# Third group of the first token part's first MLP: its in-projections by seven block products instead of eight

## The chip, the cores and the metric

The kernel runs on one core of one Trainium2 chip. The metric is the device time of one execution in microseconds (us); the median of three runs of the kernel before is 928.54 us. On the core TensorE (PE) multiplies, VectorE (DVE), ScalarE (ACT) and GpSimd (POOL) work element by element, and SyncE (SP) issues the transfers between HBM and the on-chip memory.

## The reference

Causal attention with a window of 128 (4 sequences, 8 heads, 576 positions, head dimension 64) gives 2304 tokens of 512 features; two MLPs follow, and all of it is in float32:

```python
x = attn(q, k, v)                       # 2304 x 512
g = x @ w_gate; v = x @ w_val           # 512 -> 1536
x = (g * sigmoid(g) * v) @ w_out1       # 1536 -> 512
h = x @ w_in                            # 512 -> 2048
out = (h * sigmoid(h)) @ w_out2         # 2048 -> 512
```

## The kernel before, in words

**Precision.** Every float32 operand is kept as a high and a low half in a rounded float32 format, and each product is three matmuls (high x high, high x low, low x high; L905, L906 and L907 in `passes` for the in-projections, L1188 to L1190 for the first MLP's out-projection, L1221 to L1223 for the second's). A *split* makes the halves: one rounding copy (L348 on ACT or L349 on DVE) and one subtraction (L357 on DVE or L358 on POOL).

**Tiling.** The tokens are taken in three parts of 6 tiles of 128 (768 tokens, two halves of N = 384). The hidden features of the first MLP are taken in `G1` = 6 groups of 256, those of the second in `G2` = 8 groups. A group of the first MLP has an in-projection of `w_gate` and one of `w_val`, an activation, and an out-projection that is added into `ACC`.

**Two ways for an in-projection.** With features and tokens each cut in two, the product of a group is a 2 x 2 by 2 x 2 block product.

- `moe1_plain` and `plain` do all eight block products. They read the operand slots 0 to 3 of `XOP`, which hold the plain token blocks, and four weight units per matrix. Blocks of tokens can be done as they come.
- `moe1` and `quad` do seven (the Strassen-Winograd form, products A11, S2, S1, A12, S3, S4, A22). They need slots 4, 5 and 6 of `XOP`, which hold sums and differences of blocks, and slot 1 holds a difference in place of its plain block. They need seven weight units per matrix, four of them splits of sums made by `strassen_sums` (tile `sums`). Three banks of partial results are also copied and added to one another while the products run (`copy` is L348 into `tmp`, `add_to` is L951, the fourth block is L966).

Before the first `quad` of a part, `operands` makes those slots (L695 differences into PSUM banks, then splits into `XOP`). In part 0 the attention writes `XOP` straight, so `restore` first adds the halves back into `XST` (L357 or L358, `XST<-XOP`), eight times 128x384.

**Weights.** `raw_weight` loads 512 KB of a weight matrix as it lies in HBM into one of two staging buffers `raw0`, `raw1` (L754); ACT takes some bits out of it (L755, into the single tile `top`), DVE joins them into float32 (L758, into one of three tiles `word`). Only then is the staging buffer free for the next load. A group takes six such loads (two each for `w_gate`, `w_val`, `w_out1`). Made units (ring of 17, `wu`) are stored to HBM (L772, `kept_g`, `kept_v`) so that later parts fetch them: in `quad_weights`, mode `raw` loads and makes all seven units and stores them; mode `sum` fetches the three units and two float32 words that a plain group stored, makes the other four and stores those; mode `kept` fetches all seven.

**Order of the work.** A planner (`Plan`) records every operation with a cost, a due time and its dependences, and then issues them engine by engine from this cost table; PSUM banks are handed out by it too (a bank of kind "B" for the differences, "mm" for products). Each engine, and SP for transfers, works off its list in that order. Part 1's attention is planned into the time of part 0's MLPs.

The number of plain groups is `GP`; it is used in these lines only:

```python
    moe1_plain(range(1, GP))
    restore(state["t"] - 10000.0)
    operands(XST, "xt", state["t"], plain=False)
    t_moe2 = t_next - 6000.0 + (G1 - GP) * 22 * pe_cost(6, N) + (GP - 1) * 24 * pe_cost(6, N)
    moe1(0, range(GP, G1), "raw", True)
    moe1(1, range(GP), "sum", True)
    moe1(1, range(GP, G1), "kept", True)
            if part == 1 and GP - 1 <= g < G1 - 1:
                out_sums(*jobs.pop(0), t0, gw["A22"][1])
```

`out_sums` makes, in part 1, weight sums that part 2 uses for its out-projections; there are 11 jobs, 3 of them in the first MLP with `GP` = 3 and the other 8 in the second.

Of the kernel before, what the change touches and what calls it, by code (L numbers as in the profile page):

```python
# [201 lines left out]
def attention_moe_moe2_kernel(  # L202
# [43 lines left out]
    NP = H // 2  # L246
    G1, G2 = F1 // (2 * P), F2 // (2 * P)
    EARLY = 6
    GP = 3
    NU, NO, NRAW, NW, NH, NTMP = 17, 3, 2, 3, 6, 8  # L250

    big = ctx.enter_context(tc.tile_pool(name="big", bufs=1))
# [114 lines left out]
    def pe_cost(count, n):  # L367
        return count * max(n * PE_COL + PE_MM, PE_MIN)
# [292 lines left out]
    def restore(due):  # L661

        for j in range(2):
            for blk in range(2):
                for kk in range(2):
                    c, slot = 2 * j + kk, x_slot(j, blk)
                    hi, lo = (tiles(XOP[:, slot, i, kk].bitcast(F32)) for i in range(2))
                    dst = XST[:, blk * BT:blk * BT + BT, c, :]
                    sum_op(
                        N, due, lambda dst=dst: dst, lambda hi=hi: hi, lambda lo=lo: lo, ALU.add,  # L670
                        x_keys(slot, kk), [("xt", blk * BT + t, c) for t in range(BT)],
                    )
# [175 lines left out]
    def out_weight(kind, f, first, due, load_due=None):  # L848
        i = take("o", NO)
        t, ok = O_W[i], ("o", i)  # L850
        if first:
            w, wk = raw_weight(kind, f, due if load_due is None else load_due, due + 8000.0)
            split_weight(t, ok, w, [wk], KC * P, due + 8000.0)
            store(KEPT[kind][f], flat(t), ok, ("kept", kind, f), due + 8000.0, 1460.0)
        else:
            fetch(KEPT[kind][f], flat(t), ok, ("kept", kind, f), due, 1460.0)
        return t, ok

    def out_sums(kind, g, due, behind):

        a = {}
        for j in range(2):
            n = take("word", NW)
            w, wk, low = W_R[n], ("word", n), TOP_R[0].bitcast(F32)
            for dst, dk, part in ((w, wk, 0), (low, "top", 1)):
                src = KEPT["o" + kind][2 * g + j][:, KC * P * part:KC * P * (part + 1)]
                plan.add(
                    "sp", 730.0, due + 1800.0 * j, lambda src=src, dst=dst: nc.sync.dma_start(out=dst, in_=src),
                    [("kept", "o" + kind, 2 * g + j), behind], [dk],
                )  # L870
            sum_op(KC * P, due, lambda w=w: w, lambda w=w: w, lambda low=low: low, ALU.add, ["top"], [wk])
            for i in range(2):
                a[i, j] = (w[:, 2 * P * i:2 * P * i + 2 * P], [wk])
        for n, (t, tk) in enumerate(strassen_sums(a, due, LATE)):
            m = take("stage", len(STAGE))
            u, uk = STAGE[m][0], ("stage", m)
            split_weight(u, uk, t, tk, 2 * P, due, before.pop(uk, ()), LATE)
            store(KEPT["s" + kind][g, n], lambda u=u: flat(u()), uk, ("kept", "s" + kind, g, n), due, 730.0)
# [365 lines left out]
    def flush():  # L1244
        for fn, c in pend:
            fn(state["t"])
            state["t"] += c
        pend.clear()
# [4 lines left out]
    def attention_part(part, at):  # L1253
        for i in range(part * PT, part * PT + PT):
            load(i, "k", at(i) - 14820.0)
            load(i, "q", at(i) - 20070.0)
            load(i, "v", at(i) - 7670.0)
            for halves in [(0,), (1,)] if i < EARLY else [(0, 1)]:
                t0 = at(i + 0.5 * halves[0])
                for hf in halves:  # L1260
                    prepare(i, hf, t0 - 8000.0)
                banks = score(i, halves, t0)
                for hf in halves:
                    attend(i, hf, [at(i + p / NP) for p in (2 * hf, 2 * hf + 1)], banks[hf])
                weigh(i, halves, at(i + 0.5 * halves[-1] + 1 / NP))
# [4 lines left out]
    def moe1_plain(groups):  # L1270
        for g in groups:
            if g == 0:

                gw = plain_weights("g", 0, -220.0, 26910.0)
                vw = plain_weights("v", 0, 880.0, 28010.0)
                ws = [out_weight("o1", i, True, 29750.0 - 8000.0 + 550.0 * i, 1980.0 + 550.0 * i) for i in range(2)]
                blocks = ((0, 2), (2, 2), (4, 2))
            else:
                t0 = state["t"] - WLEAD
                gw = plain_weights("g", g, t0, t0 + 8000.0)  # L1280
                vw = plain_weights("v", g, t0 + 5000.0, t0 + 5000.0 + 8000.0)
                ws = None
                blocks = ((0, BT), (BT, BT))
            for blk in blocks:
                hs = []
                n = blk[1] * P
                for i in range(2):
                    cg = plain(gw, i, blk, state["t"])
                    cv = plain(vw, i, blk, state["t"])
                    state["t"] += pe_cost(24, n)  # L1290
                    if i == 0:
                        flush()
                    if ws is None:
                        ws = [out_weight("o1", 2 * g + i, True, t0 + 12000.0 + 550.0 * i) for i in range(2)]
                    hs.append(hidden1(cg, cv, n, True, state["t"]))
                for d in range(KC):
                    pend.append((lambda due, a=(g, ws, d, blk, hs): out1(*a, due), pe_cost(6, n)))

    def moe1(part, groups, mode, psum):
        for g in groups:  # L1300
            t0 = state["t"]
            gw = quad_weights("g", g, mode, t0 - WLEAD)
            vw = quad_weights("v", g, mode, t0 - WLEAD + 7300.0)
            cg, state["t"] = quad(gw, state["t"])
            flush()
            if part == 2 and g < G1 - 1:
                units = out_units("1", g, t0 - WLEAD + 15000.0)
                cv, state["t"] = quad(vw, state["t"])
                hs = late_hidden(value1(cg, cv, state["t"]), state["t"])
                for name in ORDER_OUT:  # L1310
                    for d in range(2):
                        pend.append((lambda due, a=(g, units, hs, name, d): late_out1(*a, due), pe_cost(3, N)))
                continue
            if part == 2:
                combine(state["t"])
            ws = [out_weight("o1", 2 * g + i, part == 0, t0 - WLEAD + 15000.0) for i in range(2)]
            if part == 1 and GP - 1 <= g < G1 - 1:
                out_sums(*jobs.pop(0), t0, gw["A22"][1])
            cv, state["t"] = quad(vw, state["t"])
            hs = {}  # L1320
            for i, b in ((0, 0), (0, 1), (1, 1), (1, 0)):
                hs[i, b] = hidden1(cg[i, b], cv[i, b], N, psum, state["t"])

            for b in (1, 0):
                for d in range(KC):
                    pend.append((
                        lambda due, a=(g, ws, d, (b * BT, BT), [hs[0, b], hs[1, b]]): out1(*a, due), pe_cost(6, N),
                    ))
# [33 lines left out]
    def spread(part, t0, span):  # L1362
        attention_part(part, lambda x: t0 + (x - part * PT) / PT * span)
# [3 lines left out]
    t_next = state["t"] + 6000.0  # L1367
# [5 lines that stand above are left out]
    early = lambda x: t_next + 0.0 + (x - PT) * 33000.0  # L1373
    attention_part(1, lambda x: early(x) if x < PT + PT // 2 else t_moe2 + 20000.0 + (x - PT - PT // 2) * 33000.0)
    moe1(0, range(GP, G1), "raw", True)
    flush()
# [4 lines left out]
    spread(2, state["t"] + 6000.0, M1 + M2 - 28000.0)  # L1381
    moe1(1, range(GP), "sum", True)
    moe1(1, range(GP, G1), "kept", True)
    flush()
# [44 lines left out]
```

## Time and profile before

| | us |
|---|---|
| runs | 927.59, 928.54 (median), 932.44 |
| profiled execution, span from first to last instruction | 929.4 |
| PE busy | 909.7 (98%) |
| DVE busy | 703.4 (76%) |
| ACT busy | 529.8 (57%) |
| POOL busy | 529.0 (57%) |
| DMA, mean over the span | 260 GB/s |

Of the profiled execution the page gives the span, 929.4 us; it stands 0.9 us above the median of the runs. Matmuls overlap, so the mean duration of one (some 333 ns at 384 columns) is longer than the distance from one start to the next. PE is busy nearly all the time, so what a change does is read from PE's own work, from the few stretches in which PE is idle, and from the granted clock of TensorE (PEclk; 1.0 is 2.4 GHz, 0.5 is 1.2 GHz). In the trace part 0's first MLP runs as follows on PE: group 0 from 27 to 80 us, interleaved with the attention; group 1 to 103; group 2 (the third) to 135; groups 3, 4 and 5 to 157, 186 and 212.

### The profile page before, as it was taken

How to read it: one execution, taken by the hardware profiler on the slowest of the kernel's cores; microseconds unless marked ns; L12 is line 12 of the kernel's file. 1: busy time of each engine (PE TensorE's matmuls, PEld its weight loads, DVE VectorE, ACT ScalarE, POOL GpSimd, SP SyncE). 2: the span in 40 equal slices, each digit the busy share in tenths (PEclk: the TensorE clock that was granted, in tenths of full speed). 3: DMA queues.
4: the chain of work that ended last, by engine and by line, in shares of the span. 5: the costliest groups of instructions: out<-in, count | busy, mean ns of one | idle time of the engine just before them, and what ended most of it. 6: DMA issues, size and time to landing. Idle time of an engine off the chain costs nothing.

```text
span 929.4 us, 17799 instructions
## 1 busy us (share of the span) xinstructions
PE 909.7 (98%) x5758; PEld 845.7 (91%) x5758; DVE 703.4 (76%) x1623; ACT 529.8 (57%) x1362; POOL 529.0 (57%) x613
## 2 busy tenths in 40 slices
PE   7999999999999999999999999999999999999998
PEld 5889899997988888999999989889899999999997
DVE  7888869878989788748576977576755776868885
ACT  6887567767977685754343575445354333474431
POOL 2766377777656669675331555464344445687454
PEclk9999999999999999999999999999999999999999
DMA  9989796898888987999878787979888887587702
GB/s 226 268 236 279 251 318 210 291 304 282 272 277 284 293 293 273 331 321 309 270 246 251 251 272 272 335 268 304 287 303 249 254 250 254 190 254 229 221 24 91
DMA packets 181677, 241.58 MB, mean 260 GB/s; under 512 B 68048, under 2 KB 97232, under 8 KB 181584
## 3 DMA queue, kind: packets, MB, share of 16 engines
q1 hardware_dynamic: 181584, 240.44, 80.1%
q8 instruction: 46, 0.75, 0.3%
q14 instruction: 47, 0.39, 0.1%
HBM read 169.61 MB, written 70.78 MB: 259 GB/s over the span
## 4 chain that ended last, share of the span: by engine, by line
PE 74%; DVE 8%; POOL 6%; DMA 6%; issue 3%; ACT 2%; SPq 0%; POOLq 0%; DVEq 0%; ACTq 0%
PE bank L905 14%; PE bank L906 13%; PE bank L907 13%; PE bank L1221 5%; PE bank L1222 5%; PE bank L1223 5%; PE bank L493 3%; PE bank L607 3%; PE bank L1189 2%; PE bank L1188 2%; PE bank L1190 2%; PE bank L570 2%; POOL h L358 1%; PE bank L1121 1%; PE bank L1122 1%
## 5 line engine op out<-in xcount | busy, mean ns | idle before, releaser
L905 PE MATMUL bank<-XOP,wu 128*128 128x384 f32 (+1 forms) x868 | 297.3, 343 | 4.7 <-ACT tmp L348 1.5
L906 PE MATMUL bank<-XOP,wu 128*128 128x384 f32 (+1 forms) x868 | 289.4, 333 | 1.2 <-DVE XOP L357 0.6
L907 PE MATMUL bank<-XOP,wu 128*128 128x384 f32 (+1 forms) x868 | 289.3, 333 | 0.0
L905 PEld LDWEIGHTS bank<-XOP,wu 128*128 128x128 f32 x868 | 163.5, 188 | 14.4 <-ACT tmp L348 3.8
L906 PEld LDWEIGHTS bank<-XOP,wu 128*128 128x128 f32 x868 | 163.6, 189 | 3.5 <-DVE XOP L357 1.4
L907 PEld LDWEIGHTS bank<-XOP,wu 128*128 128x128 f32 x868 | 163.3, 188 | 0.1
L348 ACT ACTIVATE tmp<-bank 128x384 f32<-128x384 f32 x134 | 62.7, 489 | 66.0 <-PE bank L907 39.7
L358 POOL TENSOR_TENSOR h<-tmp,h 128x384 fp32r<-128x384 f32 x48 | 50.6, 1063 | 65.4 <-ACT h L348 64.3
L1221 PE MATMUL bank<-wo,h 128*128 128x512 f32 (+1 forms) x218 | 87.1, 400 | 0.1
L1223 PE MATMUL bank<-wo,h 128*128 128x512 f32 (+1 forms) x218 | 85.6, 393 | 0.0
L1222 PE MATMUL bank<-wo,h 128*128 128x512 f32 (+1 forms) x218 | 85.5, 392 | 0.0
L1233 DVE TENSOR_TENSOR ACC<-bank,ACC 128x512 f32<-128x512 f32 (+1 forms) x97 | 64.6, 681 | 17.3 <-PE bank L1223 16.6
L358 POOL TENSOR_TENSOR wu<-word,wu 128x256 fp32r<-128x256 f32 x63 | 50.7, 819 | 44.0 <-ACT wu L348 38.8
L553 POOL TENSOR_TENSOR cs<-cs,st 128x512 f32<-128x512 f32 x36 | 39.5, 1096 | 62.7 <-DVE st L550 45.5
L1188 PE MATMUL bank<-h,wo 128*128 128x384 f32 (+1 forms) x216 | 73.1, 338 | 0.1
L1189 PE MATMUL bank<-h,wo 128*128 128x384 f32 (+1 forms) x216 | 71.9, 333 | 0.9 <-POOL h L358 0.6
L951 DVE TENSOR_TENSOR bank<-bank,tmp 128x384 f32<-128x384 f32 x93 | 52.3, 562 | 26.7 <-PE bank L907 23.6
L1190 PE MATMUL bank<-h,wo 128*128 128x384 f32 (+1 forms) x216 | 71.6, 332 | 0.0
L1018 ACT ACTIVATE tmp<-bank 128x384 f32<-128x384 f32 (+1 forms) x121 | 57.3, 483 | 22.6 <-PE bank L907 10.4
L1029 DVE SCALAR_TENSOR_TENSOR bank<-tmp,bank 128x384 f32<-128x384 f32 (+1 forms) x98 | 52.7, 549 | 21.1 <-ACT tmp L1018 12.0
L348 ACT ACTIVATE h<-bank 128x384 fp32r<-128x384 f32 (+1 forms) x95 | 45.8, 484 | 39.2 <-DVE bank L1029 23.9
L758 DVE SCALAR_TENSOR_TENSOR word<-raw,top 128x512 int32<-128x512 int32 x68 | 57.8, 849 | 11.1 <-ACT top L755 10.0
(413 smaller groups left out, 2169.2 us busy)
## 6 DMA issues: line engine op xcount, KB each, us to landing
wu<-kept_i SPq DMA_DIRECT2D x112, 256.0 KB, 3.6
wu<-kept_g SPq DMA_DIRECT2D x72, 256.0 KB, 4.2
wu<-kept_v SPq DMA_DIRECT2D x72, 256.0 KB, 4.4
wo<-kept_o SPq DMA_DIRECT2D x34, 512.0 KB, 4.8
raw<-in_moe_w_out_dram SPq DMA_DIRECT2D x28, 512.0 KB, 4.9
kept_o<-wo SPq DMA_DIRECT2D x28, 512.0 KB, 4.2
kept_i<-wu SPq DMA_DIRECT2D x56, 256.0 KB, 3.2
kept_s<-later_raw SPq DMA_DIRECT2D x44, 256.0 KB, 4.3
```

The source lines that it names most:

```text
L348: act = lambda: nc.scalar.activation(out(), src(), AF.Copy)
L358: pool = lambda: nc.gpsimd.tensor_tensor(out(), x(), y(), op)
L905: nc.tensor.matmul(ps, wh, xh, start=start, stop=False, skip_group_check=True)
L906: nc.tensor.matmul(ps, wh, xl, start=False, stop=False, skip_group_check=True)
L907: nc.tensor.matmul(ps, wl, xh, start=False, stop=stop, skip_group_check=True)
L1188: nc.tensor.matmul(ps[:, 0:n], wh, h[:, 0], start=(i == 0), stop=False)
L1189: nc.tensor.matmul(ps[:, 0:n], wh, h[:, 1], start=False, stop=False)
L1190: nc.tensor.matmul(ps[:, 0:n], wl, h[:, 0], start=False, stop=(i == 1))
L1221: nc.tensor.matmul(ps, hh, wh, start=(i == 0), stop=False)
L1222: nc.tensor.matmul(ps, hh, wl, start=False, stop=False)
L1223: nc.tensor.matmul(ps, hl, wh, start=False, stop=(i == 1))
L1233: plan.add("dve", cost("dve", n), due, lambda: nc.vector.tensor_tensor(acc, pv(), acc, ALU.add), [b], keys, give=b)
```

## The change

`GP` goes from 3 to 2.

```diff
     G1, G2 = F1 // (2 * P), F2 // (2 * P)
     EARLY = 6
-    GP = 3
+    GP = 2
     NU, NO, NRAW, NW, NH, NTMP = 17, 3, 2, 3, 6, 8
```

So group 2 of part 0 goes through `moe1` with mode `raw` instead of `moe1_plain`; `restore` and `operands` of part 0 are due one group earlier; group 2 of part 1 uses mode `kept` instead of `sum`; the second half of part 1's attention is due a little earlier (`t_moe2`); and in part 1 one `out_sums` job moves from the second MLP to group 1 of the first. Everything is planned anew from there. Up to 77 us of the trace before the lists are the same but for some bank numbers; three places behind that follow. In them `h` is a group's activation, `wo` its out-projection weights, `cs` the attention's scores.

PE, from the end of group 1 to group 2; of each product or pair of products the first row. Before:

```order
L570 MATMUL bank7_135<-ident_67,cs_120 128x128 x4
L1188 MATMUL bank0_128<-h0_100,wo2_92 128x384
L1188 MATMUL bank1_129<-h0_100,wo2_92 128x384
L905 MATMUL bank4_132<-XOP_63,wu14_87 128x384
L905 MATMUL bank5_133<-XOP_63,wu16_89 128x384
L905 MATMUL bank7_135<-XOP_63,wu3_76 128x384
L1188 MATMUL bank0_128<-h2_102,wo2_92 128x384
```

And now:

```order
L570 MATMUL bank0_128<-ident_67,cs_120 128x128 x4
L1188 MATMUL bank5_133<-h0_100,wo2_92 128x384
L1188 MATMUL bank1_129<-h0_100,wo2_92 128x384
L905 MATMUL bank5_133<-XOP_63,wu14_87 128x384
L905 MATMUL bank1_129<-XOP_63,wu16_89 128x384
L905 MATMUL bank4_132<-XOP_63,wu0_73 128x384
L905 MATMUL bank3_131<-XOP_63,wu1_74 128x384
L905 MATMUL bank4_132<-XOP_63,wu3_76 128x384
L905 MATMUL bank3_131<-XOP_63,wu4_77 128x384
L905 MATMUL bank4_132<-XOP_63,wu5_78 128x384
L1188 MATMUL bank2_130<-h2_102,wo2_92 128x384
```

The first half of group 1's out-projection starts in bank 5 instead of bank 0, and the seven gate products of group 2 (wu16 and wu0 to wu5) stand where four plain products stood.

DVE, at the making of slots 4 to 6. Before:

```order
L695 TENSOR_TENSOR bank4_132<-XST_64 128x384
L695 TENSOR_TENSOR bank6_134<-XST_64,bank0_128 128x384
L349 CAST XOP_63<-bank0_128 128x384
L357 TENSOR_TENSOR XOP_63<-bank0_128,XOP_63 128x384
L357 TENSOR_TENSOR XOP_63<-bank6_134,XOP_63 128x384
L695 TENSOR_TENSOR bank3_131<-XST_64,bank4_132 128x384
```

And now:

```order
L357 TENSOR_TENSOR wo0_90<-word2_98,wo0_90 128x512
L695 TENSOR_TENSOR bank6_134<-XST_64 128x384
L758 SCALAR_TENSOR_TENSOR word2_98<-raw0_93,top0_95 128x512
L357 TENSOR_TENSOR XOP_63<-bank1_129,XOP_63 128x384
L357 TENSOR_TENSOR XOP_63<-bank2_130,XOP_63 128x384
L695 TENSOR_TENSOR bank7_135<-XST_64,bank5_133 128x384
```

The last row, which now stands behind the conversion of a `w_val` load and two splits, is the last reader of bank 5.

ACT, behind the loads of `w_out1`. Before (the loads of group 2's second half of `w_out1` and of group 3's `w_gate`):

```order
L755 ACTIVATE top0_95<-raw1_94 128x512
L348 ACTIVATE h3_103<-bank4_132 128x384
L1018 ACTIVATE tmp2_108<-bank5_133 128x384
L755 ACTIVATE top0_95<-raw0_93 128x512
L348 ACTIVATE wu7_80<-word0_96 128x256
L348 ACTIVATE wu10_83<-word0_96 128x256
L348 ACTIVATE h4_104<-bank7_135 128x384
```

And now (the first row is that of group 2's second half of `w_out1`):

```order
L755 ACTIVATE top0_95<-raw1_94 128x512
L348 ACTIVATE wu11_84<-sums_99 128x256
L348 ACTIVATE tmp2_108<-bank1_129 128x384
L348 ACTIVATE h3_103<-bank5_133 128x384
L348 ACTIVATE tmp3_109<-bank4_132 128x384
L348 ACTIVATE tmp4_110<-bank3_131 128x384
L1018 ACTIVATE tmp2_108<-bank1_129 128x384
L755 ACTIVATE top0_95<-raw0_93 128x512
```

The copies of the first seven-product form (`tmp2`, `tmp3`, `tmp4`) stand behind the bits of that load, and the bits of group 3's `w_gate` behind them.

## Rows read from the trace of the kernel before

**Rows 1.** The page: span, and each engine's busy time, share, instructions.

```profile
span 929.4 us, 17799 instructions
PE 909.7 (98%) x5758; PEld 845.7 (91%) x5758; DVE 703.4 (76%) x1623; ACT 529.8 (57%) x1362; POOL 529.0 (57%) x613
```

**Rows 2.** PE's waits over the span: us in total, times, longest.

```profile
PE bank L570 <- DVE ACC L1205: 1.4, 1, 1.4
PE bank L905 <- DVE bank L695: 1.3, 1, 1.3
PE bank L453 <- DVE KR L448: 1.2, 1, 1.2
PE bank L905 <- DVE tmp L966: 0.8, 1, 0.8
```

**Rows 3.** Stretches: length, busy PE PEld DVE ACT POOL (count), PEclk, DMA share, GB/s.

```profile
80.00:103.00 23.00, 23.00 (x165) 22.56 (x164) 21.63 (x46) 14.23 (x37) 13.88 (x16) 1.00 0.80 251
103.00:135.00 32.00, 30.43 (x189) 29.16 (x188) 20.20 (x38) 18.55 (x40) 19.91 (x25) 0.95 0.91 299
157.00:186.00 29.00, 28.25 (x200) 27.01 (x199) 26.54 (x64) 21.07 (x56) 21.95 (x27) 1.00 0.92 292
352.00:640.00 288.00, 285.73 (x1788) 264.87 (x1788) 202.11 (x484) 151.38 (x403) 153.37 (x193) 1.00 0.85 285
```

**Rows 4.** The chain that ended last, 103 to 113 us: start, length, what.

```profile
103.14 5.68 DMA raw<-in_moe_w_gate_dram
...
108.91 0.80 ACT top L755
...
109.78 0.70 DVE word L758
...
110.51 0.72 ACT wu L348 x2
...
111.64 0.57 DVE h L357
```

**Rows 5.** PE in order of time: start, duration, [idle before]; products of 384 columns.

```profile
111.46 0.66 PE L570 MATMUL bank<-ident,cs 128*128 128x128 f32 x4 [1.44 <-DVE ACC L1205]
...
114.70 0.52 PE L906 MATMUL bank<-XOP,wu 128*128 128x384 f32 x1
115.02 0.52 PE L907 MATMUL bank<-XOP,wu 128*128 128x384 f32 x1
...
134.68 0.33 PE L905 MATMUL bank<-XOP,wu 128*128 128x384 f32 x1
...
135.72 0.33 PE L905 MATMUL bank<-XOP,wu 128*128 128x384 f32 x1
```

**Rows 6.** PE in order of time, the end of the last attention tile in group 0.

```profile
83.64 0.33 PE L907 MATMUL bank<-XOP,wu 128*128 128x384 f32 x1
...
94.15 0.42 PE L1188 MATMUL bank<-h,wo 128*128 128x384 f32 x1
```

**Rows 7.** DVE in order of time.

```profile
83.71 0.42 DVE L635 TENSOR_TENSOR XOP<-bank,XOP 128x256 fp32r<-128x256 f32 x1 [0.18 <-ACT XOP L348]
...
85.85 1.50 DVE L758 SCALAR_TENSOR_TENSOR word<-raw,top 128x512 int32<-128x512 int32 x1
...
90.58 1.20 DVE L695 TENSOR_TENSOR bank<-XST 128x384 f32<-128x384 f32 x1
91.70 0.55 DVE L695 TENSOR_TENSOR bank<-XST,bank 128x384 f32<-128x384 f32 x1
```

**Rows 8.** POOL in order of time, the same stretch.

```profile
85.80 1.01 POOL L358 TENSOR_TENSOR XST<-XOP 128x384 f32<-128x384 f32 x1
...
89.37 1.99 POOL L358 TENSOR_TENSOR XST<-XOP 128x384 f32<-128x384 f32 x2
```

**Rows 9.** Groups by form over the span: busy us, mean ns, idle before.

```profile
L358 POOL TENSOR_TENSOR wu<-sums,wu 128x256 fp32r<-128x256 f32 x78 | 61.4, 816 | 1.4 <-ACT wu L348 1.1 <-DMA kept_v<-wu 0.3
L951 DVE TENSOR_TENSOR bank<-bank,tmp 128x384 f32<-128x384 f32 x93 | 52.3, 562 | 26.7 <-PE bank L907 23.6 <-ACT later_raw L348 1.4 <-ACT tmp L348 0.7
```

## The prediction

> **What bounds the kernel now.** I read the page first: PE is busy for 909.7 of 929.4 us, no other engine for more than 76% [rows 1]. The time is PE's own work, and some 20 us in which it waits. So I listed PE's waits next. Apart from the start, where the first load is awaited, only four have more than 0.7 us: 1.4, 1.3, 1.2 and 0.8 us [rows 2]. Then the stretches group by group: from 80 to 103 us PE is full and DVE nearly is (21.63 of 23 us); from 103 to 135 us, the third group, PE is idle for 1.57 us and the granted clock is 0.95 in the mean [rows 3]. In part 1 (352 to 640 us) PE is busy for 285.73 of 288 us [rows 3], so little can be won there.
>
> The wait of the third group lies at 111.46 us: PE idles 1.44 us, and the matmuls after it start 0.32 us apart (114.70, 115.02) where later ones need 1.04 us for six, 0.173 us each (134.68 to 135.72) [rows 5]. That is the lower level of TensorE's clock, 1.2 GHz in place of 2.4 GHz, after an idle engine. The chain tells what PE waited for. A load of `w_gate` for group 3, which nobody needs before 135 us, takes 5.68 us; then ACT takes its bits (0.80) and DVE joins them (0.70); only behind these stand ACT's copies and the last step of `h`, which PE needs [rows 4]. Urgent work stood behind a conversion of weights that were not urgent.
>
> **The change part by part.**
>
> *Matmuls.* Eight block products per matrix become seven. A block product is 2 x 3 matmuls of 384 columns, and there are two matrices: 12 matmuls fewer, at 0.173 us [rows 5]. PE is full around them, so all of it counts: **-2.1 us**.
>
> *The old wait and its slow clock.* In the new lists of PE and ACT (the change, above) the seven gate products, 7.3 us of PE work, stand where this wait came up, and the activation that was awaited there no longer exists in that place. I take the 1.44 us as gone. The slow clock costs (1 - 0.95) x 32 = 1.6 us [rows 3]. Together **-3.0 us**; the other bound is 0, if a wait as long takes its place.
>
> *The end of the last attention tile.* Six products of 384 columns (1.04 us) that covered the wait for DVE's last low half now come later. That half ends at 83.71 + 0.42 us; on the new list DVE has one restoring addition and one difference more ahead of it, while POOL has one addition less, so some 0.4 us later, 84.5 us. PE is there at 83.64 + 0.17 = 83.8 us [rows 6, 7]: **+0.7 us**, between 0 and 1.5.
>
> *The bank of the differences.* Group 1's first out-projection opens bank 5. Its last reader is now DVE's difference for slot 4. I laid DVE's list after 84.5 us row by row (0.34 us for 256 columns, 0.47 for 384, 0.6 to 0.7 for 512, from starts in [rows 7]; waits for ACT where ACT's list is longer): that difference ends at about 96 us. PE came there at 94.15 us [rows 6], and with 0.7 us of delay at 94.9 us. **+1.0 us**; if nothing on DVE is late it is 0, and if each difference there needs 1.20 instead of 0.55 us [rows 7], it is near 3.
>
> *The first seven-product form.* Its copies stand on ACT behind the bits of a `w_out1` load (the change, above). By the same working that load is issued at some 101.5 us and lands near 106 us; the bits and one copy of 0.4 us end at 107.4, while the first product has ended at 105.8. Copy, add (0.56 [rows 9]), copy end near 109.0 us, PE wants to go on at 108.5: **+0.6 us**. The bounds are 0 and 2.2, which is the load landing 1.7 us later, as the 5.68 us one in [rows 4]. From about 1.4 us on I add the slow clock's 1.6 us, since 1.44 us brought it and the waits of 1.3 and 1.2 us [rows 2] did not (the stretch 157 to 186 us, with one of 0.8, has 1.00 too [rows 3]). I give that 2 in 10 over all three waits: **+0.3 us**.
>
> *Weights made in part 0 instead of part 1.* Eight sums and six more splits move into 80 to 135 us: on POOL 14 x 0.82 = 11.5 us [rows 9], where it is busy for 33.8 of 55 us [rows 3]; ACT has room as well. In part 1 the same goes away and two splits with it, which covers nothing PE waited for: 0. Four stores of 256 KB move the same way. They are 1.05 MB, at 299 GB/s 3.5 us of transfer, in a stretch whose DMA share is 0.91 [rows 3]; the total is the same. Group 2's first sums are ready near 97 us, PE needs them at 104 us; those of `w_val` near 106, needed near 119. Group 4's first load comes behind seven stores now, near 133 us instead of 126, and PE needs what is made of it (about 14 us later) near 153. So 6 us of cover remain; without it a wait there starts. I take 0.
>
> *The seven-product form's own work.* Six copies of 0.49 us on ACT, and on DVE four L951 and two L966 of 0.56 us [rows 9], 3.4 us beside PE's work in a stretch where DVE is idle for 11.8 of 32 us [rows 3]: 0.
>
> *The moved `out_sums` job and part 2.* The same instructions, in stretches without waits of weight: 0, give or take 1 us for another mix of order.
>
> Sum: -2.1 - 3.0 + 0.7 + 1.0 + 0.6 + 0.3 = **-2.5 us**. Against the profiled execution that is 929.4 - 2.5 = 926.9 us; the median of the runs stands 0.9 us lower, so I forecast **926.0 us**.
>
> **A rule of the skill.** DVE's difference took 1.20 us at 90.58 us while POOL added from 89.37 to 91.36 us, and 0.55 us right after; L758 took 1.50 us beside POOL's addition at 85.80 [rows 7, 8]. The Trainium skill (SBUF — State Buffer, on the shared port pair) has a rule that speaks against this change: a DVE instruction with two SBUF inputs and a GpSimd one exclude each other for the whole instruction. The trace agrees, with 0.65 us lost once. By it DVE would pay for POOL's additional sums and splits; what that makes of the time is rival 3, worked out there from the rows.
>
> **The rivals.**
>
> 1. *The wait goes and nothing takes its place.* For it: each of my three new waits is small beside what its working can be off. Against it: DVE is full up to 103 us [rows 3]. -2.1 - 3.0 = -5.1 us: 923.4 us. Chance 0.20.
> 2. *No gain.* The first seven-product form stops for 2.2 us behind the load, TensorE falls to 1.2 GHz again, and bank 5 costs 1 us: -5.1 + 0.7 + 1.0 + 2.2 + 1.6 = +0.4, 928.9 us. For it: the same shape of wait is there now. Chance 0.20.
> 3. *Slower: DVE falls behind.* Up to 103 us it has 1.4 us of room [rows 3]. POOL gets 14 instructions of 0.82 us more [rows 9]; if half of them hold a DVE instruction up for their whole length, as the addition at 89.37 did for most of its own [rows 7, 8], DVE loses 5.7 us. Bank 5 and slot 4 come that much later, PE stops for 1.0 + 5.7 us with the slow clock after it (1.6), and the late loads of `w_val` and `w_out1` stop the first form by 2.2 us and its clock by 1.6: -5.1 + 0.7 + 6.7 + 1.6 + 2.2 + 1.6 = +7.7, 936.2 us. It decides from some 3 us of delay on DVE at 96 us. Against it: only 4 us of POOL's additional work falls before 97 us, and POOL waits for DVE in between. Chance 0.13.
> 4. That the change doesn't do what it says is excluded: the lists have 12 matmuls fewer.
>
> **How the numbers follow.** Forecast 0.47, rivals 0.20, 0.20, 0.13. A measurement of this kernel tells 0.5%, 4.6 us, from no change: faster is below 923.9, slower above 933.2 us. Faster 0.20 (rival 1), same 0.67 (forecast and rival 2), slower 0.13 (rival 3). The range goes from 922.0 (rival 1, and the smaller waits of 0.8 and less in groups 4 and 5 gone with it) to 932.0 (rival 2 with bank 5 at its bound of 3 and 1 us for the order); rival 3 is left out.
>
> **What would show it.** PE's instructions 5746, its busy time near 907. No slow clock between 103 and 135 us. PE idle 0.5 to 1 us near 84 us, before the first out-projection of group 1 near 95 us (released by DVE's L695), and before the fourth gate product of group 2 near 109 us (released by ACT's copy `tmp`). Group 3's first product starts 3 to 4 us earlier, counted at equal work. The forecast is wrong if PE waits for a weight unit in groups 2 to 5, if a stretch of slow clock stands after 80 us, or if part 1 or 2 differ by more than 1 us.

## The result and the profile after

The changed kernel takes 933.74 us in the median of 16 runs (931.21 to 937.12); the kernel before, measured beside it, 929.17 us (927.45 to 932.44, 16 runs). The ratio is 1.0051 with a 95% interval of 1.0037 to 1.0064: slower by 4.6 us, where 926.0 us and a range of 922 to 932 were forecast. The profiled execution of after spans 933.0 us, where [rows 1] has 929.4; a run's time stands 1.7 us above its span.

The page of after, its span and busy times:

```profile
span 933.0 us, 17789 instructions
PE 906.5 (97%) x5746; PEld 842.1 (90%) x5746; DVE 715.9 (77%) x1636; ACT 527.8 (57%) x1365; POOL 523.9 (56%) x605
```

PE has the 12 matmuls less and is busy for 3.2 us less than in [rows 1] (one slow stretch of its clock less is part of that), and the span is 3.6 us longer. So the loss is idle PE, not work. PE's waits over the span (us in total, times, longest):

```profile
PE bank L905 <- ACT tmp L348: 4.1, 5, 1.8
...
PE bank L905 <- DVE tmp L349: 1.8, 2, 1.0
...
PE bank L905 <- ACT XOP L348: 1.7, 2, 1.3
PE bank L905 <- DVE tmp L966: 1.5, 4, 0.7
PE bank L1188 <- DVE bank L695: 1.2, 1, 1.2
...
PE bank L607 <- POOL u L584: 1.0, 1, 1.0
```

The one wait of 1.4 us of [rows 2] is gone. In its place stand seven of 0.8 us or more behind group 0, four of them for a copy (`tmp`) that a seven-product form wants. Where they lie, the stretches tell (length, busy PE PEld DVE ACT POOL, PEclk, DMA share, GB/s; this execution reaches the same work some 2 us earlier than that of before, because a slow stretch of TensorE's clock near 20 us, in code that the change leaves alone, is missing from it):

```profile
78.00:101.00 23.00, 20.94 (x148) 19.62 (x147) 21.09 (x53) 15.91 (x46) 15.76 (x20) 1.00 0.67 223
101.00:131.50 30.50, 29.47 (x208) 28.20 (x207) 23.64 (x54) 23.54 (x62) 26.11 (x34) 1.00 0.96 319
...
154.00:183.00 29.00, 28.79 (x197) 26.60 (x196) 26.95 (x64) 20.98 (x59) 20.09 (x25) 1.00 0.91 290
250.00:260.00 10.00, 8.19 (x37) 7.42 (x36) 7.04 (x13) 7.54 (x19) 2.43 (x4) 0.83 0.82 283
350.00:638.00 288.00, 284.10 (x1775) 264.08 (x1773) 205.48 (x484) 148.05 (x396) 148.25 (x183) 1.00 0.85 286
```

Beside [rows 3]: the third group has 1.00 of the clock now and 1.03 us of idle PE, but the stretch ahead of it lost 2.06 us where there was nothing, and at 250 us, in part 0's second MLP, PE idles 1.81 us and the clock falls to 0.83 in the mean. Group 4 idles less (0.21 us in the third row, 0.75 in [rows 3]), a wait of 0.97 us for POOL (L584) is new at 201.40 us, in group 5, and part 1 idles 3.9 us where it idled 2.3. These are the PE rows (start, duration, [idle before]):

```profile
82.87 0.38 PE L906 MATMUL bank<-XOP,wu 128*128 128x256 f32 x1 [0.47 <-DVE XOP L635]
...
95.05 0.45 PE L1188 MATMUL bank<-h,wo 128*128 128x384 f32 x1 [1.24 <-DVE bank L695]
...
122.69 0.45 PE L905 MATMUL bank<-XOP,wu 128*128 128x384 f32 x1 [1.03 <-ACT tmp L348]
...
252.82 0.44 PE L905 MATMUL bank<-XOP,wu 128*128 128x384 f32 x1 [1.81 <-ACT tmp L348]
...
254.63 0.52 PE L905 MATMUL bank<-XOP,wu 128*128 128x384 f32 x1
254.95 0.52 PE L906 MATMUL bank<-XOP,wu 128*128 128x384 f32 x1
...
531.73 0.44 PE L905 MATMUL bank<-XOP,wu 128*128 128x384 f32 x1 [1.30 <-ACT XOP L348]
```

From 254.33 us on the starts are 0.32 us apart for 3.41 us, 1.2 GHz again, as in [rows 5], in another place.

To see when the time goes, I counted PE's rows in each trace from a common one (the end of its 24th row of L445, at 52.2 us in before and 50.2 us in after) to the same numbered row further on. Negative means that the kernel is ahead of before, in us:

| up to (us in before) | what ends there | after | one stretch moved | attention due as before | before, attention due earlier |
|---|---|---|---|---|---|
| 173 | 65 rows of L1188, the start of group 4's out-projection | -1.4 | -1.8 | -1.9 | +0.2 |
| 217 | 96 rows of L1188, the end of group 5's out-projection | -1.1 | -1.1 | -1.0 | -0.9 |
| 236 | the first row of the second MLP's out-projections | -2.1 | -2.0 | -2.0 | -0.8 |
| 266 | a quarter of them | +2.0 | -0.1 | -0.7 | +0.9 |
| 303 | half of them | +3.0 | +0.9 | -0.1 | +1.8 |
| 402 | 24 rows of L1188 in part 1 | +5.1 | +2.3 | +2.4 | +1.7 |
| 545 | the first such row of part 1 | +5.9 | +3.4 | +2.4 | +2.2 |
| end | | +5.6 | +3.4 | +2.3 | +1.5 |

(The last three columns are experiments below. At 173 and 217 us and from 266 us on the three kernels with two plain groups have done the same work as before but for the 12 matmuls; at 236 us two short rows of L445 are still to come in them.) Up to 236 us the change is ahead, by 1.1 to 2.1 us where -2.5 was the sum. Then, in 30 us, it gives back 4.1, and 3.6 more up to the end. What happened at 252.8 us is in the chain that ended last (start, length, what; the first five rows), beside a second place at 528 us:

```profile
248.54 1.12 DVE wo L357
...
249.69 1.42 DVE word L758
...
251.67 0.76 ACT top L755
252.43 0.34 ACT tmp L348
...
252.82 0.44 PE bank L905
...
522.87 4.85 DMA top<-kept_o
...
527.74 0.69 DVE word L357
528.43 0.48 DVE ACC L1205
...
528.93 0.58 DVE bank L695
```

At 248.5 us DVE splits and joins `w_out2`, and only then adds the partial result that PE needs; ACT has its own share of `w_out2` ahead of the copy. It is the pattern of [rows 4], urgent work behind a conversion, in a stretch where the kernel before had no wait at all. At 528 us DVE waits for a fetch that an `out_sums` conversion wants, and the sums and differences of part 1 stand behind it.

### The profile page after: what moved, and what is told of

Read it like the earlier page. It is cut to its first block, busy times and chain, and to the rows that moved or that the text cites. A ratio compares the mean times of both kernels' runs of the same rounds, so it can differ in the third digit from the quotient of the medians.

```text
span 933.0 us, 17789 instructions
## 1 busy us (share of the span) xinstructions
PE 906.5 (97%) x5746; PEld 842.1 (90%) x5746; DVE 715.9 (77%) x1636; ACT 527.8 (57%) x1365; POOL 523.9 (56%) x605
## 4 chain that ended last, share of the span: by engine, by line
PE 64%; DVE 16%; DMA 7%; POOL 5%; ACT 4%; issue 3%; SPq 0%; DVEq 0%; ACTq 0%; POOLq 0%
PE bank L905 12%; PE bank L907 11%; PE bank L906 11%; PE bank L1221 5%; PE bank L1223 5%; PE bank L1222 5%; DVE word L758 2%; PE bank L493 2%; PE bank L607 2%; DVE bank L695 2%; PE bank L1188 2%; PE bank L1190 2%; PE bank L1189 2%; DVE XOP L357 2%; DVE bank L520 1%
## 5 line engine op out<-in xcount | busy, mean ns | idle before, releaser
L905 PE MATMUL bank<-XOP,wu 128*128 128x384 f32 (+1 forms) x864 | 296.5, 343 | 10.4 <-ACT tmp L348 4.1
L905 PEld LDWEIGHTS bank<-XOP,wu 128*128 128x128 f32 x864 | 162.7, 188 | 21.9 <-ACT tmp L348 7.0
L348 ACT ACTIVATE tmp<-bank 128x384 f32<-128x384 f32 x137 | 63.8, 487 | 65.9 <-PE bank L907 41.1
L358 POOL TENSOR_TENSOR h<-tmp,h 128x384 fp32r<-128x384 f32 x48 | 49.5, 1041 | 69.0 <-ACT h L348 67.3
L951 DVE TENSOR_TENSOR bank<-bank,tmp 128x384 f32<-128x384 f32 x97 | 54.5, 561 | 28.3 <-PE bank L907 24.1
L553 POOL TENSOR_TENSOR cs<-cs,st 128x512 f32<-128x512 f32 x36 | 40.3, 1120 | 62.8 <-DVE st L550 35.8
L1188 PE MATMUL bank<-h,wo 128*128 128x384 f32 (+1 forms) x216 | 73.2, 339 | 1.2 <-DVE bank L695 1.2
L348 ACT ACTIVATE h<-bank 128x384 fp32r<-128x384 f32 (+1 forms) x94 | 45.2, 483 | 42.3 <-DVE bank L1029 25.4
L758 DVE SCALAR_TENSOR_TENSOR word<-raw,top 128x512 int32<-128x512 int32 x68 | 60.6, 891 | 9.5 <-ACT top L755 7.3
L533 ACT ACTIVATE cs<-cs,st 128x128 f32<-128x128 f32 x144 | 56.3, 394 | 19.3 <-DVE st L527 19.1
```

Source lines behind the costliest of these rows:

```text
L348: act = lambda: nc.scalar.activation(out(), src(), AF.Copy)
L758: lambda: nc.vector.scalar_tensor_tensor(w.bitcast(I32), word, 13, top, ALU.logical_shift_right, ALU.bitwise_or),
L905: nc.tensor.matmul(ps, wh, xh, start=start, stop=False, skip_group_check=True)
L1188: nc.tensor.matmul(ps[:, 0:n], wh, h[:, 0], start=(i == 0), stop=False)
```

## Experiments

Two theories stood at the start. **A**: the time is lost in a handful of waits where the new order puts urgent additions and copies behind conversions. **B**: from 236 us on DVE and the two staging buffers can't deliver, whatever the order. A third came later, **C**: a loss that belongs to two plain groups under any plan.

**One stretch of the order moved.** In the changed kernel the operations are recorded, six of them are moved, and all are issued: at 253 us the low half of `w_out2`, the join, the next load, its bits and the high half go behind the addition and the copy.

```diff
+MOVES = [([1646, 1651, 1652, 1656, 1658, 1663], 1665)]
+        order = list(range(len(self.log)))
+        for who, behind in MOVES:
+            order = [i for i in order if i not in who]
+            at = order.index(behind) + 1
+            order[at:at] = who
```

> The changed kernel, with one thing moved: in the second MLP of part 0, third group, DVE's add into the second bank (L951) and ACT's copy that follows it are issued ahead of the conversions of two w_out2 halves that stood in front of them; every other instruction keeps its order. Theory A (the loss is a handful of waits in which the urgent adds and copies of a seven-product form stand behind weight conversions, at places that the new plan happens to give): PE's wait of 1.8 us at 252.8 us and the 3.4 us of slow clock after it go, the time falls by 2.5 to 3.5 us against the changed kernel, to about 930.5 to 931. Theory B (the second MLP is late because DVE and the two staging buffers cannot keep up since sums and splits moved into part 0): the wait comes up again within the same group or the next, the time stays within 1 us of the changed kernel.

932.04 us, ratio to before 1.0031 [1.0014, 1.0047]. Its profile (lines stand 9 higher: L960 is L951, L767 is L758), DVE at that place:

```profile
249.66 0.56 DVE L960 TENSOR_TENSOR bank<-bank,tmp 128x384 f32<-128x384 f32 x1 [1.14 <-ACT tmp L357]
250.14 0.68 DVE L366 TENSOR_TENSOR wo<-word,wo 128x512 fp32r<-128x512 f32 x1
250.85 0.69 DVE L767 SCALAR_TENSOR_TENSOR word<-raw,top 128x512 int32<-128x512 int32 x1
```

and PE there, and the span with its mean clock:

```profile
253.26 0.44 PE L914 MATMUL bank<-XOP,wu 128*128 128x384 f32 x1 [1.14 <-ACT tmp L357]
```

```profile
core 0: 930.7 us, clock 1.000
```

The addition starts at 249.66 instead of 251.02, the wait falls from 1.81 to 1.14 us, the slow stretch is gone, and the span is 2.3 us shorter (2.5 to 3.5 expected). The median fell by 1.7 us only, and the interval overlaps that of the changed kernel (1.0037 to 1.0064). The conversions take 0.68 and 0.69 us here, 1.20 and 1.41 us in the changed kernel, where POOL works beside them (its rows stand further down). A holds for this wait as the profile shows it.

**The kernel before with its own wait repaired.** The conversion of group 3's `w_gate`, which stood ahead of group 2's `h` [rows 4], goes behind it.

```diff
+MOVES = [([689, 692, 694, 696, 698, 699, 703, 705, 708], 707)]
```

> The kernel before, with one thing moved: the conversion of group 3's first w_gate half in part 0 (ACT's bits, DVE's join, what hangs on them) is issued behind ACT's and DVE's last steps of the activation half that PE waited for at 111.5 us; all else keeps its order. Theory A: the wait of 1.44 us and the slow clock after it go, and the time falls by about 3.0 us to 926. Theory B says the same of this place, since no DVE load moved here; if the wait only moves a few us on, both would expect less than 1 us.

929.30 us, ratio 0.9996 [0.9982, 1.001]: a miss. PE waited 1.63 us at 113.35 us instead, for DVE's accumulation; that execution had no slow clock after it. With the conversion out of the way, the next thing that PE needs came up.

**The due time of part 1's attention.** `GP` also shifts `t_moe2`, 2.1 us earlier. The first kernel is that of before with the earlier due time, the second the changed one with the old due time.

```diff
-    t_moe2 = t_next - 6000.0 + (G1 - GP) * 22 * pe_cost(6, N) + (GP - 1) * 24 * pe_cost(6, N)
+    t_moe2 = t_next - 6000.0 + (G1 - 2) * 22 * pe_cost(6, N) + (2 - 1) * 24 * pe_cost(6, N)
```

(in the second kernel 3 in place of 2.)

> The kernel before (GP = 3, no group changed), only the due time of the second half of part 1's attention 2.1 us earlier, as the changed kernel has it. Theory A: the plan of part 0's second MLP comes out in another order, so the time moves by 1 to 5 us, more likely up, though no work was moved; waits of over 0.7 us between 220 and 320 us in other places than before. Theory B: within 1 us of the kernel before.

> The changed kernel with that due time 2.1 us later, as the kernel before has it. Theory A: the order from 230 us on is another one, the time moves by 1 to 4 us from the changed kernel's, and the wait at 252.8 us changes its length or place. Theory B: within 1 us of the changed kernel, 933 to 934.5.

929.98 us, ratio 1.0004 [0.9988, 1.002], and 931.01 us, ratio 1.0014 [0.9997, 1.003]. The first moved by less than 1 us, as B expected and not A; the second by more, as A expected and not B. In the second, no wait is left at 253 us; of PE's waits for ACT's copies this is the row:

```profile
PE bank L905 <- ACT tmp L348: 1.9, 5, 0.6
```

4.1 us with a longest of 1.8 in after, 1.9 with 0.6 here. The same seven-product groups, with one due time 2.1 us later, are 2.7 us faster in the medians (0.37% by the ratios). What is lost at 253 us belongs to the order, and a small number in the plan brings it or takes it away.

**Four stretches moved by hand**, at 95, 123, 253 and 292 us.

```diff
+MOVES = [([608, 614, 623], 624),
+         ([975, 978, 979, 985, 986, 988], 987),
+         ([1646, 1651, 1652, 1656, 1658, 1663, 1666], 1668),
+         ([1889, 1893, 1894, 1897, 1899], 1900)]
```

> The changed kernel with four stretches of the lists written by hand: at each, a conversion of weights (with the next load and what follows from it) is put behind the urgent piece that stood behind it: the difference that frees bank 5 (95 us), the first copy and addition of group 3 (123 us), the addition and both copies of the second MLP's third group (253 us), and those of its fourth (292 us). Theory A (the time is lost where urgent additions and copies stand behind conversions): these four waits, 1.2, 1.0, 1.1 and 1.0 us in the run with one stretch moved, fall to under 0.5 us each, and 2 to 4 us go: 928 to 930 us, a ratio of 0.999 to 1.001. Theory B (the second MLP is late because DVE and the staging buffers cannot deliver, whatever the order): PE waits for weight units instead, the sum of the waits stays, 931 to 934 us.

936.06 us, ratio 1.0088 [1.0064, 1.0112]: the clearest miss. Two of the four waits fell (95 us: 1.24 to 0.31; 253 us: to 0.59), two did not (123 us: 1.01; 292 us: 0.99), and others came up. Its chain at the first new one, and at 525 us (lines stand 12 higher: L360 is L348, L917 is L905):

```profile
146.09 4.92 DMA raw<-in_moe_w_val_dram
...
151.21 0.70 ACT wu L360 x2
151.91 0.39 ACT tmp L360
...
152.34 0.44 PE bank L917
...
524.94 7.31 DMA top<-kept_o
...
532.27 0.69 DVE word L369
```

At 152 us, where the changed kernel has no wait, the load of `w_val` lands at 151.01 us, the copy stands behind two splits that follow it, and PE waits 1.20 us. A conversion put off also puts off the next load into its staging buffer; that the two moved ones at 95 and 123 us made this load late is likely, but no run shows it by itself. At 525 us the fetch for `out_sums` takes 7.31 instead of 4.85 us, DVE stands before it, and PE waits 1.94 and 2.33 us there. So A in its simple form, each wait a separate loss that a move gives back, falls.

**The `out_sums` job left in the second MLP.**

```diff
-            if part == 1 and GP - 1 <= g < G1 - 1:
+            if part == 1 and GP <= g < G1 - 1:
```

> The changed kernel with the out_sums job left where it was before the change (none in group 1 of part 1's first MLP). The order is the changed kernel's up to the second part. If the moved job is what costs the 1.4 us from 303 to 402 us and the 0.8 us up to 545 us: 931 to 932 us. If those are other waits of the new order: 933 to 934.5 us, the changed kernel's time.

934.52 us, ratio 1.0062 [1.0038, 1.0086]. The 1.30 us at 531.7 us is gone from its profile and a wait of 1.63 us stands at 463 us instead. The runs don't show the moved job to cost the time.

**The conversions of `w_out2` due later**, by 4, 6 and 8 us, each with two and with three plain groups. The work is the same as in the changed kernel or in the one before, and only the order differs. Theory A's ranges for these runs are 3 to 7 us wide, so it is B and C that they test.

```diff
-            ws = [out_weight("o2", 2 * g + i, mode == "raw", t0 - WLEAD + 7300.0) for i in range(2)]
+            ws = [out_weight("o2", 2 * g + i, mode == "raw", t0 - WLEAD + (13300.0 if mode == "raw" else 7300.0)) for i in range(2)]
```

(13300 is 6 us later; 11300 and 15300 are 4 and 8.)

> The changed kernel with the conversions of w_out2 in part 0's second MLP due 6 us later in the plan, so that in the lists fewer of them stand ahead of additions and copies; the sister run is the kernel before with the same due time. Theory A: the wait at 253 us and its slow clock are gone, 928 to 931 us. Theory B: the conversions come too late or as late as ever, PE waits for w_out2, 932 us or more, and the sister run is faster by 2 us or more.

> The kernel before (three plain groups) with the same later due time of w_out2. It tells how far the planner's order alone moves the time. Theory A and mere scatter of orders: within 2 us of 929.2 either way, and the changed kernel with that due time between 2.5 us faster and 2 us slower. Theory B: 929 us or less, with the changed kernel 2 us or more above it.

> The changed kernel with the conversions of w_out2 in part 0's second MLP due 4 us later in the plan: another order of the same work. Theory A (the change's own stage gives some 2 us, and the order that the planner makes of the rest moves the time by some 3 us either way): 927 to 934 us, and 177 us into the kernel (the end of group 3) still 1.5 to 2.5 us ahead of the kernel before, counted from a common matmul. Theory C (a loss that belongs to two plain groups, whatever the order): over the sister run with three plain groups by 2 us or more, as the changed kernel over the kernel before.

> The kernel before with the conversions of w_out2 due 4 us later. Theory A: 928 to 933 us, as the run with 6 us later, which was slower than the kernel before by 0.32% with the same work. Theory C: 928 to 930 us, and the changed kernel with that due time 2 us or more above it.

> The changed kernel with the conversions of w_out2 due 8 us later. Theory A: 927 to 934 us; against its sister run anywhere from 5 us faster to 4 us slower, and the mean of the five pairs of equal due times between 2 us faster and 1.5 us slower. Theory C: 2 us or more above its sister run.

> The kernel before with the conversions of w_out2 due 8 us later. Theory A: 928 to 933 us. Theory C: 928 to 930 us.

Of the single runs, three plain groups with 6 us (931.82 us) missed its range of 2 us around 929.2; the others lie within A's ranges. With the two due times of the attention this makes five pairs that differ in `GP` alone. Ratios to the kernel before (those measured have intervals of about ±0.0015):

| setting | three plain groups | two plain groups | difference |
|---|---|---|---|
| attention due as in before | 1 | 1.0014 | +0.14% |
| attention due 2.1 us earlier | 1.0004 | 1.0051 (the change) | +0.47% |
| `w_out2` due 4 us later | 0.9996 | 1.0013 | +0.17% |
| 6 us later | 1.0032 | 1.0020 | -0.12% |
| 8 us later | 1.0023 | 1.0031 | +0.08% |
| mean | 1.0011 | 1.0026 | +0.15% |

The middle column is the reading: the same work, planned with one number changed, spreads over 0.36%, 3.3 us, and the intervals of its ends (0.9979 to 1.0013 and 1.0016 to 1.0047) don't meet. The one beside it spreads over as much. The change by itself, the mean of the differences, costs 1.4 us, with 0.9 us as its standard error (the five scatter by 0.21%); a 95% interval from five such differences goes from -1.1 to +3.8 us. So it is no sure loss, and less than the 4.6 us measured. In one pair it is even the faster one. These 4.6 us are 0.15% from the change, 0.25% because this plan is the worst of the five with two plain groups, and 0.11% because the kernel before lies below the mean of its own five. B falls with the 6 us pair and the 4 us one, where two plain groups take 930.4 and 930.1 us. C in its form (2 us or more over the sister run in each pair) falls too.

The traces of the five pairs say where two plain groups gain and lose. At 217 us, where each pair has done the same work but for the 12 matmuls, they are 1.0 us, 0.2 us and 0.5 us ahead in three pairs and 0.2 and 3.5 us behind in two, +0.4 us in the mean. PE has idled 1.2 to 4.2 us longer with them in every pair, 2.1 us in the mean (4.6 against 2.5 us since the common row), as much as the 12 matmuls save. So something of C is left: in each plan tried, two plain groups pay for the saved matmuls with idle PE in part 0's first MLP.

No version beat the kernel before: the best, three plain groups with 4 us, has 928.75 us, ratio 0.9996 [0.9979, 1.0013].

**Slow stretches of the clock, counted.** Every run lists its span and mean granted clock, and a stretch of 3.41 us at half speed lowers that mean by 0.0018. By this the kernel before has 1.09 such stretches in each of the 89 executions that the experiments list (one more, with a mean of 0.948 and a usual span, is left out), the changed one 1.37 (16), and that with one stretch moved 0.41 (12). Within a kernel each goes with some 1.3 us more. So, as an estimate, after and before differ by 0.4 us through the clock and by 4.4 without it; of the 2.1 us that the moved stretch wins in the mean span, some 1.2 are the clock.

## Why the prediction was wrong

By its own steps:

- *Matmuls, -2.1 us.* Right in the count: 5746 matmuls. PE is busy for 906.5 us where near 907 was given, but the two profiles also differ by a slow stretch, which the prediction books under the next step.
- *The old wait and its slow clock, -3.0.* The wait is gone, as said, and in the profiles the slow stretch with it. But the 1.6 us came from one execution, and that one had two slow stretches where the mean is 1.09. For the median it was sized too high, and the changed kernel has such stretches elsewhere. The wait itself is a matter of the plan too: in the other runs with three plain groups it has 0.44 to 1.77 us, and of the five profiles with three in the pairs two have a slow stretch behind it. The other slow stretch stands behind a wait that the prediction's list and [rows 2] leave out, the longest after the first load, at 20.44 us:

```profile
PE bank L570 <- POOL cs L553: 1.7, 1, 1.7
```

- *End of the last attention tile, +0.7.* 0.47 us at 82.87 us, released by DVE's L635 as said.
- *Bank 5, +1.0.* 1.24 us at 95.05 us, released by L695. Why it is no less, DVE's rows show:

```profile
90.15 1.27 DVE L357 TENSOR_TENSOR wo<-word,wo 128x512 fp32r<-128x512 f32 x1 [0.36 <-ACT wo L348]
91.35 1.10 DVE L695 TENSOR_TENSOR bank<-XST 128x384 f32<-128x384 f32 x1
92.36 1.23 DVE L758 SCALAR_TENSOR_TENSOR word<-raw,top 128x512 int32<-128x512 int32 x1
...
248.46 1.20 DVE L357 TENSOR_TENSOR wo<-word,wo 128x512 fp32r<-128x512 f32 x1
249.69 1.41 DVE L758 SCALAR_TENSOR_TENSOR word<-raw,top 128x512 int32<-128x512 int32 x1
251.02 0.55 DVE L951 TENSOR_TENSOR bank<-bank,tmp 128x384 f32<-128x384 f32 x1
```

  and POOL's beside them:

```profile
90.14 0.74 POOL L358 TENSOR_TENSOR sums<-word,word 128x256 f32<-128x256 f32 x1
90.84 1.19 POOL L358 TENSOR_TENSOR sums<-word,sums 128x256 f32<-128x256 f32 x1
91.98 2.90 POOL L358 TENSOR_TENSOR wu<-sums,wu 128x256 fp32r<-128x256 f32 x3
...
248.09 1.02 POOL L358 TENSOR_TENSOR h<-tmp,h 128x384 fp32r<-128x384 f32 x1 [0.18 <-ACT h L348]
249.06 1.49 POOL L553 TENSOR_TENSOR cs<-cs,st 128x512 f32<-128x512 f32 x1
```

  At 90 to 93 us each of the three takes 0.5 to 0.6 us longer than the 0.69 us (512 columns, in the run with one stretch moved) and 0.55 us (384, [rows 7]) that such instructions take, while POOL makes the added sums. That is rival 3's mechanism, with some 1.7 us on DVE instead of 5.7. The kernel's time came near that rival's 936.2 us, but not by its way: there is no wait of 6.7 us and no slow clock in the first MLP.
- *First seven-product form, +0.6 near 109 us.* No wait there. The same pattern stands one group later, 1.03 us at 122.69 us: ACT takes 0.80 us for the bits of a load and splits a unit ahead of the copy. It stands in all eight profiles with two plain groups (0.6 to 1.5 us), as does that at 95 us (1.2 us in seven, 0.31 with the four moves). The step looked at the first form only.
- *Sum for this stage, -2.5.* -1.4 at 173 us and -1.1 at 217 us in this pair, and over the five pairs -0.5 and +0.4 in the mean. The sign held here; the size did not, because the new waits up to 217 us come to 3.7 us (0.47, 1.24, 1.03, 0.97) where 2.3 were given, and the old wait with its slow clock is worth less in the other plans.
- *Weights made earlier, 0.* No wait for a weight unit in groups 2 to 5, as said. But the wait at 201.40 us, for POOL's L584, is not in the sum. It stands in seven of the eight profiles with two plain groups (0.9 to 1.1 us, 0.26 in the eighth) and in none of the six with three. In the chain ACT's input to it comes behind the bits of a `w_in` load that takes 6.61 us; that the weights made earlier bring that load late is not shown.
- *"The moved `out_sums` job and part 2. The same instructions, in stretches without waits of weight: 0, give or take 1 us for another mix of order."* **This step failed.** From 217 us, the end of part 0's first MLP, to the end it was +6.7 us in the profiles. Part 0's second MLP was not even named in it. That the stretch had no waits was taken as a quality of the work; it was one of the order. In the five pairs the plans of the same work have waits of 0.7 to 1.3 us there with three plain groups and of up to 1.8 us with two, and the times of either five spread over 3.3 us or more. A term of 0 with ±1 us was the mis-sized one: by the plans tried it should have had ±2 and, as the kernel before lies 0.11% below the mean of its five, a mean 1 us above zero.

What stays open: whether the mean loss of 1.4 us differs from zero, and how much of the idle PE behind 217 us belongs to two plain groups. In the profiles of the pairs they lose 1.6 us more from there to the end, in the mean, with four of the five losing. No run took these stages apart with the order held fixed.

## What to carry to other kernels

Where a planner writes the order, an edit re-rolls everything behind it: cost the edit by its stage, and then add the spread that a few harmless changes of due times give, measured, before a gain of that size is believed or given up. Judge such an edit by pairs, several settings with and without it, not by one kernel against one, and compare their traces where both have done the same work. And a wait repaired by hand moves the next load: look further on what that made late.

## What the runs showed of the hardware

- Length of an idle stretch alone does not tell if TensorE's clock falls. In the 14 profiles, while PE had work, the granted clock fell to 1.2 GHz 12 times at the end of a wait of 1.44 to 2.33 us or up to 1.5 us behind it, and twice by a shorter wait with a second one close by (1.15 and 0.43 us at 221.7 us, 1.31 and 0.42 us at 528.9 us, both with two plain groups and 4 us). It did not fall after waits of 1.47, 1.70 and 1.74 us, and of four waits of 1.63 us two brought it and two did not. So the 1.4 us from which the prediction adds the slow clock is no bound. The slow stretch was 3.41 us long each time.
- DVE's split and join of `w_out2` took 1.20 and 1.41 us beside POOL's L358 and L553 at 248 to 251 us, and 0.68 and 0.69 us in the run with one stretch moved, where they ran after 250.1 us. POOL's L553 took 1.49 us there and 1.04 us in that run, so the two engines held each other up. What stands ahead of urgent work can so be twice as long as its usual row.
